# Casting x on GpSimd in place of VectorE, one slot sooner, with two of the four loads placed two slots behind the casts

## Chip, cores, metric

One Trainium2 chip, one core. The metric is device time in microseconds (us), the median of several executions. A profile is one further execution, and its span is about 1.8 us shorter than the time of the same run, as the time includes more than first to last instruction.

## The reference, cut to what matters

```python
# x: (8, 3008, 256) fp32
X = np.fft.rfft(x, axis=1)                       # along the 3008 positions
Y = X * (filt_r + 1j * filt_i)[None, :, :]
x = np.fft.irfft(Y, n=3008, axis=1).reshape(24064, 256)
h = np.maximum(x @ moe_w_in, 0.0)                # 256 -> 2048
out = h * h @ moe_w_out                          # 2048 -> 256
```

## The kernel before

The feed-forward part runs in groups of 512 tokens, 8 slots to a group. Into the slots of one batch the Fourier part of the next is woven: x is loaded, cast to fp16, transformed (psA), multiplied by the filter (psB to prod to yf), transformed back (psP), and later written out as yt (psY). TensorE works through all of this in program order; so does VectorE. I call the stretch from a batch's first psB to its last psP the **filter stage**; a *stage length* below is the time from one batch's first psB to the next batch's first psB, read from TensorE's timeline.

```python
def cast_x(b, c, eng=nc.vector):
    t = p_x16.tile([94, 8, D], F16, tag="x16", name=f"x16_{b}_{c}")
    eng.tensor_copy(out=t, in_=x32s.pop((b, c))[0:94])      # L340
    x16s[(b, c)] = t
...
def unit_b(b, p):                                # 12 units p in a batch
    ps = psF(f"psB_{b}_{p}")                     # psF: two PSUM buffers, for psA, psB, psP, psY
    ... two psB matmuls ...
    nc.vector.tensor_mul(out=prod, in0=ps (from PSUM), in1=sF[...])      # L453
    nc.vector.tensor_copy(out=yf[0:64], in_=prod[64:128, 1])             # L460
    nc.vector.tensor_copy(out=yf[64:128], in_=prod[0:64, 1])             # L461
def unit_s(b, p):
    nc.vector.tensor_add(out=yf, in0=prod[:, 0], in1=yf)                 # L467
def ffn_sq(g, s):                                # once in every slot
    nc.vector.tensor_mul(out=v, in0=v, in1=v)    # L570, h squared
...
def fft_plan(b):                                 # put(slot, place, function, ...)
    t0 = 14 if b == 1 else 19
    for p in range(12):
        r = t0 + (17 if b == 1 else 18) * p // 11
        put(r, 0, unit_b, b, p)
        put(r, 0, unit_s, b, p)
        put(r + 2, 1, unit_p, b, p)              # the psP pair that reads yf
    t0 = 34 if b == 1 else 40
    for c in range(4):
        put(t0, 1, read_z, b, c)                 # dZ -> zt, which psY needs
    if b + 1 < B:
        for c in range(2):
            put(t0 - 13, 1, load_x, b + 1, c)    # two input buffers x32
        for c in range(4):
            r = t0 - 8 + 3 * c
            put(r, 1, cast_x, b + 1, c)
            if c < 2:
                put(r, 1, load_x, b + 1, c + 2)
```

So batch 1's stage carries the casts of batch 2's x, and so on: six stages with four casts each.

## Time and profile before

| | before |
|---|---|
| time, median of 3 runs | 793.43 us (793.39 to 793.74) |
| profiled span | 791.9 us |
| stage length, batch 1; batches 2 to 6 | 92.39; 94.94 each |
| from the last batch's first psB to the start of the last psO | 147.80 us |
| VectorE busy, of it casts (L340) | 550.3 us, 29.2 |

How to read it: stages 2 to 6 agree to 0.01 us because TensorE streams in them without a wait. Whatever lengthens a stage is therefore TensorE waiting, and it can be read off stage by stage.

### The profile page before, as it was taken

What the parts mean: (1) busy time and instruction counts of PE and PEld (TensorE: products, weight loads), DVE (VectorE), ACT (ScalarE), POOL (GpSimd) and SP (SyncE); (2) the same over time, 40 slices, a digit from 0 to 9 for tenths busy, and PEclk for the clock granted to TensorE, in tenths of its full rate; (3) what the DMA queues carried; (4) which work ended last, traced back from release to release, by engine and by line L of the source; (5) the groups of instructions that cost most, each with busy time, mean ns of one, the idle gap of its engine ahead of it and who ended that gap; (6) DMA issues with size and microseconds to landing.
All of it is one profiled execution on the core that took longest, in us unless ns stands there. A gap on an engine that the chain in (4) does not pass through costs nothing.

```text
span 791.9 us, 14822 instructions
## 1 busy us (share of the span) xinstructions
PE 778.9 (98%) x6102; PEld 552.5 (70%) x6102; DVE 550.3 (69%) x897; ACT 557.4 (70%) x711; POOL 23.6 (3%) x36
## 2 busy tenths in 40 slices
PE   8989999999999999999999999999999999999998
PEld 5746667667676777867777676776767677676666
DVE  6866994579755897559965699556995579553342
ACT  3976776777777777767776777676777777776664
POOL 3800000000000000000000000000000000000000
PEclk9999999999999999999999999999999999999999
DMA  9994554346814557154562555424563332611111
GB/s 363 368 260 153 146 157 111 93 135 167 205 42 112 167 155 180 48 173 135 132 167 65 163 147 155 112 80 148 159 180 86 97 133 66 147 40 41 41 41 54
DMA packets 88571, 107.32 MB, mean 136 GB/s; under 512 B 6336, under 2 KB 79040, under 8 KB 84288
## 3 DMA queue, kind: packets, MB, share of 16 engines
q1 hardware_dynamic: 88296, 106.19, 46.5%
q8 instruction: 48, 0.79, 0.4%
q10 hardware_dynamic: 144, 0.18, 0.1%
q14 instruction: 19, 0.16, 0.1%
q0 software_dynamic: 64, 0.00, 0.0%
HBM read 58.12 MB, written 48.23 MB: 134 GB/s over the span
## 4 chain that ended last, share of the span: by engine, by line
PE 89%; DVE 6%; DMA 3%; ACT 1%; SPq 0%; issue 0%; DVEq 0%; ACTq 0%
PE psO L579 40%; PE psH L562 38%; PE psA L361 3%; PE psY L532 2%; PE psB L445 2%; DMA f<-in_filt_i_dram 2%; PE psP L496 2%; DVE prod L453 2%; DVE h L570 1%; DMA wout<-in_moe_w_out_dram 1%; PE psf L287 1%; PE psf L290 1%; DVE yf L467 0%; ACT sF L298 0%; DVE yf L461 0%; ACT h L566 0%
## 5 line engine op out<-in xcount | busy, mean ns | idle before, releaser
L566 ACT ACTIVATE h<-psH 128x1024 f16<-128x1024 f32 x376 | 384.9, 1024 | 189.3 <-PE psH L562 186.7
L579 PE MATMUL psO<-sWout,h 128*128 128x256 f16 x3008 | 388.9, 272 | 0.6 <-DVE h L570 0.6
L562 PE MATMUL psH<-yt,sWin 128*128 128x512 f16 (+7 forms) x1728 | 386.9, 351 | 1.6 <-DVE yt L541 0.7
L579 PEld LDWEIGHTS <-h 128*128 128x128 f16 x3008 | 290.6, 98 | 79.1 <-DVE h L570 0.9
L570 DVE TENSOR_TENSOR h<-h 128x1024 f16<-128x1024 f16 x376 | 252.6, 685 | 104.7 <-ACT h L566 104.5
L562 PEld LDWEIGHTS <-sWin 128*128 128x128 f16 x1728 | 159.5, 98 | 101.7 <-issue 3.3
L453 DVE TENSOR_TENSOR prod<-psB,sF 128x1024 f16<-128x1024 f32 x84 | 102.3, 1218 | 2.8 <-PE psB L445 2.8
L541 DVE CAST yt<-psY 128x376 f16<-128x376 f32 x62 | 34.0, 549 | 59.4 <-PE psY L532 59.4
L367 DVE CAST u<-psA 96x512 f16<-96x512 f32 x50 | 34.3, 687 | 47.3 <-PE psA L361 45.1
L498 ACT CAST ze<-psP 128x512 f16<-128x512 f32 x84 | 49.1, 585 | 17.2 <-PE psP L496 14.7
L590 ACT COPY ost<-psO 128x512 f32<-128x512 f32 (+1 forms) x96 | 55.8, 581 | 6.8 <-PE psO L579 5.3
L532 PE MATMUL psY<-sC,zt 112*128 112x94 f16 x512 | 42.4, 205 | 1.4 <-DMA zt<-dZ 1.4
L532 PEld LDWEIGHTS <-zt 112*128 112x128 f16 x512 | 35.1, 98 | 11.6 <-issue 1.6
L467 DVE TENSOR_TENSOR yf<-prod,yf 128x512 f16<-128x512 f16 x84 | 35.7, 425 | 2.9
L361 PE MATMUL psA<-x,sC 94*96 94x512 f16 x96 | 36.6, 382 | 0.0
L445 PE MATMUL psB<-ut,sSB 128*128 128x256 f16 x192 | 36.5, 273 | 0.0
L496 PE MATMUL psP<-yf,sSP 128*128 128x256 f16 x168 | 32.1, 272 | 0.5 <-DVE prod L453 0.3
L539 ACT CAST yt<-psY 128x376 f16<-128x376 f32 x66 | 30.9, 468 | 2.0 <-issue 1.7
L445 PEld LDWEIGHTS <-sSB 128*128 128x128 f16 x192 | 18.5, 98 | 19.5
L340 DVE CAST x<-x 94x2048 f16<-94x2048 f32 x24 | 29.2, 1216 | 0.0
L365 ACT CAST u<-psA 96x512 f16<-96x512 f32 x50 | 28.6, 572 | 0.0
L460 DVE COPY yf<-prod 64x512 f16<-64x512 f16 x84 | 24.3, 289 | 2.9
(65 smaller groups left out, 253.2 us busy)
## 6 DMA issues: line engine op xcount, KB each, us to landing
x<-in_x_dram SPq DMA_DIRECT2D x20, 768.0 KB
zt<-dZ SPq DMA_DIRECT2D x64, 192.0 KB
dU<-u SPq DMA_DIRECT2D x28, 384.0 KB
dZ<-ze SPq DMA_DIRECT2D x28, 384.0 KB
out_dram<-ost SPq DMA_DIRECT2D x66, 128.0 KB
out_dram<-ost SPq DMA_DIRECT2D x31, 256.0 KB
ut<-dU SPq DMA_DIRECT2D x7, 1024.0 KB
xw<-in_x_dram SPq DMA_DIRECT2D x6, 1024.0 KB
```

The source lines that it names most:

```text
L361: nc.tensor.matmul(ps[0:96, :], sSA, x16s[(b, c)][:, m, :], start=True, stop=True)
L445: nc.tensor.matmul(ps[:, i * D:(i + 1) * D], sSB[:, 2 * p + i, :], uts[b][:, 2 * p + i, :], start=True, stop=True)
L453: nc.vector.tensor_mul(out=prod, in0=ps.rearrange("p (a d) -> p a d", d=D).unsqueeze(1).to_broadcast([128, 2, 2, D]), in1=sF[:, :, 2 * p:2 ...
L467: nc.vector.tensor_add(out=yf, in0=prod[:, 0], in1=yf)
L496: nc.tensor.matmul(ps[:, i * D:(i + 1) * D], sSP[:, 2 * p + i, :], yf[:, i, :], start=True, stop=True)
L498: nc.scalar.copy(out=zes[(b, c)][:, 2 * i6:2 * i6 + 2, :], in_=ps.rearrange("p (a d) -> p a d", d=D))
L532: nc.tensor.matmul(ps[:, 94 * jj:94 * jj + 94], zt[:, 4 * (g % 2) + jj, dt * 128:(dt + 1) * 128], sSY, start=True, stop=True)
L562: nc.tensor.matmul(ps[:, i, o:o + n], sWin[:, dt, jt * 128:(jt + 1) * 128], yts[b][:, dt, r:r + n], start=(dt == 0), stop=(dt == 1))
L566: nc.scalar.activation(out=h2[:, 2 * s:2 * s + 2, :], in_=ps, func=AF.Relu)
L570: nc.vector.tensor_mul(out=v, in0=v, in1=v)
L579: nc.tensor.matmul(pso[g][:, t % 2, :], h2s[g][:, jt, t * 128:(t + 1) * 128], sWout[:, jt, :], start=(jt == 0), stop=(jt == NJT - 1))
L590: nc.scalar.copy(out=ost[:, h0:h0 + step, :], in_=pso[g][:, h0:h0 + step, :])
```

## The change

The intent: take 29 us of casts off VectorE, which is nearly full in the filter stage, and give them to GpSimd, which is idle after the first 40 us; and place the third and fourth loads so that SyncE no longer waits for a cast.

```diff
-    def cast_x(b, c, eng=nc.vector):
+    def cast_x(b, c, eng=nc.gpsimd):
...
             for c in range(4):
-                r = t0 - 8 + 3 * c
+                r = t0 - 9 + 3 * c
                 put(r, 1, cast_x, b + 1, c)
                 if c < 2:
-                    put(r, 1, load_x, b + 1, c + 2)
+                    put(r + 2, 1, load_x, b + 1, c + 2)
```

## The prediction

> **What bounds the kernel now.** I read the page's busy shares first, then TensorE's waits over the whole run, then its waits from 120 us on, then the busy time of each engine in one stretch, and last the timelines of VectorE, TensorE, GpSimd and SyncE around one set of casts.
>
> ```profile
> PE 778.9 (98%) x6102; PEld 552.5 (70%) x6102; DVE 550.3 (69%) x897; ACT 557.4 (70%) x711; POOL 23.6 (3%) x36
> ...
> L340 DVE CAST x<-x 94x2048 f16<-94x2048 f32 x24 | 29.2, 1216 | 0.0
> ...
> PE psH L562 <- DVE yt L541: 0.2, 1, 0.2
> ...
> 165.60:206.70 41.10, 41.10 (x298) 29.04 (x297) 39.71 (x71) 30.37 (x38) 0.00 (x0) 1.00 0.50 140
> 206.70:260.50 53.80, 53.80 (x440) 38.16 (x439) 30.11 (x48) 38.17 (x51) 0.00 (x0) 1.00 0.45 127
> ```
>
> The first line says TensorE is busy 98% of the span. The third is the entire answer to "what does TensorE wait for between 120 and 790 us": one wait of 0.2 us. In that stretch it streams without a gap: in its timeline the group of 8 psO products takes 0.87 us from its start to the next start, the group of 4 psH products the same, a psB or psP pair 0.22, and they follow each other exactly. So the end is set by TensorE, and there is next to nothing to win. The last two lines (columns: length, then busy TensorE, weight load, VectorE, ScalarE, GpSimd) add the one danger: in the 41.1 us in which batch 2's filter stage (psB to prod to yf to psP) runs, VectorE is busy 39.71 us, 97%; in the 53.8 us after it, only 56%. VectorE is a second bound that is almost reached once per batch, and that is where the x casts (line L340, 24 of 1.216 us) sit.
>
> How near is it? Here is VectorE around the casts of batch 3's x, and after it the TensorE pairs that wait for it:
>
> ```profile
> 183.84 0.42 DVE L467 TENSOR_TENSOR yf<-prod,yf 128x512 f16<-128x512 f16 x1
> 184.19 0.69 DVE L570 TENSOR_TENSOR h<-h 128x1024 f16<-128x1024 f16 x1
> 184.79 1.22 DVE L453 TENSOR_TENSOR prod<-psB,sF 128x1024 f16<-128x1024 f32 x1
> 186.04 0.29 DVE L460 COPY yf<-prod 64x512 f16<-64x512 f16 x1
> 186.34 0.29 DVE L461 COPY yf<-prod 64x512 f16<-64x512 f16 x1
> 186.66 0.42 DVE L467 TENSOR_TENSOR yf<-prod,yf 128x512 f16<-128x512 f16 x1
> ...
> 194.14 1.22 DVE L340 CAST x<-x 94x2048 f16<-94x2048 f32 x1
> ...
> 205.72 0.42 DVE L467 TENSOR_TENSOR yf<-prod,yf 128x512 f16<-128x512 f16 x1
> ...
> 188.67 0.38 PE L496 MATMUL psP<-yf,sSP 128*128 128x256 f16 x2
> ...
> 206.27 0.38 PE L496 MATMUL psP<-yf,sSP 128*128 128x256 f16 x2
> ```
>
> The yf that is added at 186.66 (ready at 187.09) is read by the psP pair at 188.67: a margin of 1.58 us. After two casts (194.14 and 201.51) the stage's last yf is ready at 206.15 and read at 206.27: 0.12 us is left. The same margins, to 0.02 us, come back in the stages at 281 to 301, 376 to 396, 471 to 491 and 566 to 586 us. So before the change the schedule just fits.
>
> **What the Trainium skill says.** "SBUF — State Buffer", section "Who interferes with whom": GpSimd has only VectorE's second port pair; it is an exclusive lock held for a whole instruction, against VectorE copies and casts in a two-port mode and against a VectorE operation with two SBUF inputs; an operation with one SBUF input outside those modes does not contend. "VectorE: DVE Perf Modes", section "Mode 2×_2P", gives that mode to single-source copies from SBUF to SBUF. The trace of before agrees where it can be tested, in the prologue:
>
> ```profile
> 11.61 0.69 DVE L222 CAST xw<-xw 128x1024 f16<-128x1024 f32 x1 [1.20 <-DMA xw<-in_x_dram]
> 11.64 1.56 POOL L222 CAST xw<-xw 128x1024 f16<-128x1024 f32 x1 [8.98 <-DMA xw<-in_x_dram]
> 20.49 1.04 POOL L222 CAST f<-f 128x1024 f16<-128x1024 f32 x1 [2.37 <-DMA f<-in_filt_i_dram]
> 20.56 1.51 DVE L222 CAST f<-f 128x1024 f16<-128x1024 f32 x1 [0.26 <-DMA f<-in_filt_i_dram]
> 24.42 7.06 DVE L453 TENSOR_TENSOR prods<-psB,sF 128x1024 f16<-128x1024 f32 x6
> 35.15 3.99 POOL L222 CAST xw<-xw 128x1024 f16<-128x1024 f32 x4
> ```
>
> At 11.6 VectorE came first by 0.03 us and GpSimd's 1.0 us cast took 1.56; at 20.5 GpSimd came first and VectorE's 0.69 us cast took 1.51, about the 0.8 us that it had to wait. The product from PSUM ran at 7.06/6 = 1.18 us beside GpSimd's copies, undisturbed. No pair of a tensor_tensor with two SBUF inputs (L467, L570) and a GpSimd operation is in this trace. "GPSIMD Engine Reference", section "Engine selection", has one-input work on GpSimd at roughly line rate; the trace agrees: 0.998 us for 1024 elements (3.99/4).
>
> **The change part by part.** *Removed:* 24 casts x 1.216 = 29.2 us of VectorE, four for each of six batches. At most they free the waits for VectorE up to 120 us: 0.59 us at 114.2 (psO for h, after a late chain of casts at 101 to 109) and 0.27 at 93.9, say 0.9 us together. After 120 us they free nothing, as there is no wait.
> *Added:* 24 casts on GpSimd. From 1024 elements at 0.998 us and 1504 at 1.41 (2.82/2), the slope is 0.86 ns per element, so 2048 take 0.998 + 1024 x 0.00086 = 1.88 us undisturbed (estimate). 24 x 1.88 = 45 us on an engine that was idle after 40 us: no bound by itself.
> *Moved:* on GpSimd the program slot no longer sets when a cast runs, since nothing else is queued there: it runs when its load lands. The first two loads are issued at 177.97 and just after (SyncE's timeline); their packets and semaphores land at about 184.2 and 186.8. So the first two casts move from 194.1 and 201.5 to about 184.3 and 186.8. The third load was issued at 195.38, on the end of the first VectorE cast; its buffer is now free since about 186, so SyncE passes it right after the output write of 191.5, and the fourth right after the dZ write of 197.5 instead of 202.75. "Two slots later" therefore means earlier or equal in time, and SyncE's 49 us of waits for L340 vanish (41.9 + 7.2 in its own waits). They were on no path, so this is worth nothing.
>
> *What the lock costs in one stage.* The first cast asks at 184.3 while L570 runs, gets the pair at 184.8 and holds it to 186.7. L453 (PSUM) is not held up until 186.0; then L460 waits 0.62 us, starting at 186.66. The second cast asks at 186.85 and gets the pair at the end of L460, at 186.95, to 188.83: L461 waits 1.87 us. The yf that had 1.58 us of margin is late by 0.62 + 1.87 - 1.58 = 0.9 us, and its psP pair, in order before everything else on TensorE, stalls it by about 1.0 us. The next units had margins of 2.07 and 2.27 us and now 1 us more, so no second stall. At 194 to 206 VectorE is without its two casts (-2.4 us) and gets two lock waits of 0.7 to 1.9 us: about even against the 0.12 us margin, which has grown by the earlier stall. So 1.0 us a stage, in the five stages of batches 2 to 6: 5 us. The stage of batch 1, whose first unit margins at 93 to 98 us are 2.2 to 2.9 us, costs 0 to 0.7.
> Sum: 793.4 - 0.9 + 0.4 + 5.0 = 798 us.
>
> **The rivals.** *The casts are hidden:* GpSimd asks for the pair while VectorE issues back to back, and if VectorE keeps it until its next product from PSUM, the hold of 1.88 us lies beside 1.22 us that needs no pair; only 0.66 us is lost per cast, 1.3 for two, under the 1.58 margin. Then nothing stalls: 793.4 - 0.9 = 792.5. For it: the prologue shows who came first, not who wins when VectorE's queue is full; and tensor_tensor may not block at all. Against it: the blocked casts there started as soon as the pair was free. *A worse lock:* each cast blocks VectorE for its full 1.88 us and the last unit's margin of 0.12 fails as well: another 1 to 1.5 us per stage, so 804. Against it: the prod, 42% of a unit's VectorE time (1.22 of 2.9 us), needs no pair. *x comes late for psA:* the fourth load would land at about 203 and psA needs it only in the next batch, 20 us later and more (the psA products of batch 3 start at 234); excluded. *VectorE was the bound and the 29 us show:* that would be 764; the empty list of waits excludes it.
>
> **Range and chances.** I give the lock with stalls (798) about 0.5, the hidden casts (792.5) 0.4, the worse lock (804) 0.1: 0.5 x 798 + 0.4 x 792.5 + 0.1 x 804 = 796.4. As either of the first two is likelier in a half measure than in full, I put the point at 795.5 us and the range at 792.0 to 801.0. Faster by 2% needs 777.6, under what TensorE streams: 0.01. Slower by 2% needs 809.3, that is 2.7 us in each of six stages: 0.04.
>
> **What would show it.** In the profile after: GpSimd at about 68 us (9%), the L340 group on POOL with a mean of 1.9 to 2.4 us; VectorE's L460, L461, L467 and L570 with means above 289, 289, 425 and 685 ns (the blocked ones), L453 unchanged; new TensorE waits of about 1 us, five times, of psP L496 on DVE L467, near 189, 284, 379, 474 and 569 us; SyncE's wait on L340 gone. It is wrong if VectorE's means do not move (no lock for tensor_tensor), if the waits stand near 206 us instead (the end of the stage), if the GpSimd cast is far longer than 1.9 us, or if no wait appears.

## More of the kernel before

The page's lines of VectorE's filter work, to be compared later (columns: busy us, mean ns of one, then idle before):

```profile
L570 DVE TENSOR_TENSOR h<-h 128x1024 f16<-128x1024 f16 x376 | 252.6, 685 | 104.7 <-ACT h L566 104.5
L467 DVE TENSOR_TENSOR yf<-prod,yf 128x512 f16<-128x512 f16 x84 | 35.7, 425 | 2.9
L460 DVE COPY yf<-prod 64x512 f16<-64x512 f16 x84 | 24.3, 289 | 2.9
```

## The result, and the profile after

805.22 us, median of 4 runs (803.43 to 806.85), against 793.59 for before on the same chip. The ratio is 1.0143, 95% interval 1.0117 to 1.0169. A ratio here is always the mean time of one kernel's runs over that of the other's in the same rounds, so not quite the ratio of the quoted medians. The change makes the kernel 1.4% **slower**: clear of the noise and above the predicted range (792.0 to 801.0).

| stage | before | after | longer by |
|---|---|---|---|
| batch 1 | 92.39 | 94.45 | 2.06 |
| 2 | 94.94 | 96.80 | 1.86 |
| 3 | 94.94 | 97.46 | 2.52 |
| 4 | 94.94 | 96.87 | 1.93 |
| 5 | 94.94 | 96.86 | 1.92 |
| 6 | 94.94 | 96.65 | 1.71 |
| rest, from the last batch's first psB | 147.80 | 147.80 | 0.00 |

The six stages that carry casts hold 12.0 us of it, two each; the rest, without a cast, holds nothing. The profiled spans differ by 13.1 us; the other 1.1 lie before the first stage, where this execution had 3.4 us of TensorE at half clock (granted 0.92 between 36 and 52 us, against 1.00). The profile of the kernel with late GpSimd casts (below), which is no slower than before, shows one as well (granted 0.96), so it is no part of the effect.

The page after, in answer to the lines above:

```profile
PE 784.0 (97%) x6102; PEld 552.3 (69%) x6102; DVE 553.0 (69%) x873; ACT 557.6 (69%) x711; POOL 72.0 (9%) x60
...
L570 DVE TENSOR_TENSOR h<-h 128x1024 f16<-128x1024 f16 x376 | 267.8, 725 | 116.3 <-ACT h L566 113.4
L453 DVE TENSOR_TENSOR prod<-psB,sF 128x1024 f16<-128x1024 f32 x84 | 102.2, 1217 | 1.5 <-PE psB L445 1.4
L340 POOL CAST x<-x 94x2048 f16<-94x2048 f32 x24 | 48.4, 2015 | 514.9 <-DMA x<-in_x_dram 482.9
...
L467 DVE TENSOR_TENSOR yf<-prod,yf 128x512 f16<-128x512 f16 x84 | 43.9, 523 | 2.9
...
L460 DVE COPY yf<-prod 64x512 f16<-64x512 f16 x84 | 29.2, 348 | 2.9
```

VectorE runs 24 instructions fewer (873 against 897) and is busy *longer*: 553.0 against 550.3 us. L570 grew by 15.2 us, L467 by 8.2, L460 by 4.9 and L461 by 1.6 (25.8 against 24.2): 29.9 us, or **1.25 us of VectorE time for each GpSimd cast, where its own cast had cost 1.216**. L453, which reads one operand from PSUM, did not move. GpSimd's cast takes 1.89 us undisturbed and 2.02 on average. Read cast by cast, each of the 24 overlaps exactly one VectorE operation that is over 0.1 us longer than the median of its kind: 11 L570, 7 L460, 5 L467 and 1 L461.

Now TensorE's waits over the whole run; the list of before has neither of these two (columns: total us, times, longest):

```profile
PE psB L445 <- DVE prod L453: 6.5, 8, 1.1
...
PE psP L496 <- DVE yf L467: 2.5, 4, 1.5
```

And the chain of one loss, batch 2's stage, from the timelines of GpSimd, VectorE and TensorE:

```profile
187.58 2.19 POOL L340 CAST x<-x 94x2048 f16<-94x2048 f32 x1 [71.84 <-DMA x<-in_x_dram]
190.41 2.02 POOL L340 CAST x<-x 94x2048 f16<-94x2048 f32 x1 [0.64 <-DMA x<-in_x_dram]
...
189.19 0.73 DVE L460 COPY yf<-prod 64x512 f16<-64x512 f16 x1
...
190.59 2.98 DVE L570 TENSOR_TENSOR h<-h 128x1024 f16<-128x1024 f16 x2
193.50 1.21 DVE L453 TENSOR_TENSOR prod<-psB,sF 128x1024 f16<-128x1024 f32 x1
...
196.91 1.22 DVE L453 TENSOR_TENSOR prod<-psB,sF 128x1024 f16<-128x1024 f32 x1
...
198.18 0.38 PE L445 MATMUL psB<-ut,sSB 128*128 128x256 f16 x2 [1.08 <-DVE prod L453]
```

Both casts start when their loads have landed, not in their slots. Counted from the stage's first psB (165.64 before, 168.78 after), they stand at 18.8 and 21.6 us, where VectorE had run them at 28.5 and 35.9 (194.14 and 201.51). The first holds L460 up by 0.44 us; the second catches one of two L570 operations (2.98 us for the two, against 1.29). The prod that should follow at once starts at 193.50; its psB had ended at 191.10. Two units later the tenth unit's psB, one slot behind the ninth's, finds its buffer still being read by the prod of 196.91 to 198.13, and TensorE stands. The line gives 1.08 us of idle time; a pair that does not wait begins 0.17 us before the modelled end of the one in front, so this wait costs the stage 1.25 us. Before, the same prod ran from 191.91 to 193.13 and that psB started at 193.66, with 0.53 us to spare:

```profile
191.91 1.23 DVE L453 TENSOR_TENSOR prod<-psB,sF 128x1024 f16<-128x1024 f32 x1 [0.20 <-PE psB L445]
...
193.66 0.38 PE L445 MATMUL psB<-ut,sSB 128*128 128x256 f16 x2
```

### The profile page after: what moved, and what is told of

It is laid out like the page before. It is cut to its first block, busy times and chain, and to the rows that moved or that the text cites. A ratio compares the mean times of both kernels' runs of the same rounds, so it can differ in the third digit from the quotient of the medians.

```text
span 805.0 us, 14863 instructions
## 1 busy us (share of the span) xinstructions
PE 784.0 (97%) x6102; PEld 552.3 (69%) x6102; DVE 553.0 (69%) x873; ACT 557.6 (69%) x711; POOL 72.0 (9%) x60
## 4 chain that ended last, share of the span: by engine, by line
PE 71%; DVE 26%; ACT 1%; issue 1%; DMA 1%; ACTq 0%; DVEq 0%; SPq 0%
PE psO L579 30%; PE psH L562 30%; DVE prod L453 9%; DVE h L570 8%; DVE yf L467 4%; DVE yf L460 3%; PE psA L361 3%; PE psY L532 3%; DVE yf L461 2%; PE warm L268 1%; PE psB L445 1%; PE psP L496 1%; PE psf L287 1%; PE psf L290 1%; ACT sF L298 0%
## 5 line engine op out<-in xcount | busy, mean ns | idle before, releaser
L570 DVE TENSOR_TENSOR h<-h 128x1024 f16<-128x1024 f16 x376 | 267.8, 725 | 116.3 <-ACT h L566 113.4
L453 DVE TENSOR_TENSOR prod<-psB,sF 128x1024 f16<-128x1024 f32 x84 | 102.2, 1217 | 1.5 <-PE psB L445 1.4
L340 POOL CAST x<-x 94x2048 f16<-94x2048 f32 x24 | 48.4, 2015 | 514.9 <-DMA x<-in_x_dram 482.9
L467 DVE TENSOR_TENSOR yf<-prod,yf 128x512 f16<-128x512 f16 x84 | 43.9, 523 | 2.9
L532 PEld LDWEIGHTS <-zt 112*128 112x128 f16 x512 | 35.1, 98 | 11.2 <-issue 1.2
L445 PE MATMUL psB<-ut,sSB 128*128 128x256 f16 x192 | 36.5, 272 | 6.5 <-DVE prod L453 6.5
L460 DVE COPY yf<-prod 64x512 f16<-64x512 f16 x84 | 29.2, 348 | 2.9
```

Of the source, the lines that this page charges most:

```text
L445: nc.tensor.matmul(ps[:, i * D:(i + 1) * D], sSB[:, 2 * p + i, :], uts[b][:, 2 * p + i, :], start=True, stop=True)
L453: nc.vector.tensor_mul(out=prod, in0=ps.rearrange("p (a d) -> p a d", d=D).unsqueeze(1).to_broadcast([128, 2, 2, D]), in1=sF[:, :, 2 * p:2 ...
L532: nc.tensor.matmul(ps[:, 94 * jj:94 * jj + 94], zt[:, 4 * (g % 2) + jj, dt * 128:(dt + 1) * 128], sSY, start=True, stop=True)
```

## The experiments

In the sketches of edits, "after" is the changed kernel. Where a kernel has added lines in `cast_x`, later line numbers are higher by 2 (L570 becomes L572). Losses of a stage are given for batches 2 to 6 against 94.94 us.

The theory after seeing the result: **GpSimd's cast holds the SBUF port pair of the prediction's lock, which VectorE's copies and two-input operations need, so VectorE loses as much time as its own cast had cost, but in lumps of up to 1.9 us and earlier in the stage, where a psB or psP has less margin.** Rivals: the moved loads and slots; any fixed cost of work on GpSimd; the mere removal of the casts from VectorE's order.

### All but the engine

```diff
 after:
-    def cast_x(b, c, eng=nc.gpsimd):
+    def cast_x(b, c, eng=nc.vector):
```

> The whole change but the engine: the casts one slot sooner and the loads two slots after them, on VectorE as before. Theory (GpSimd's casts hold VectorE's second port pair beside the filter stage): within 1.5 us of before, 792 to 795, filter stages of 94.9 us. Rival (the moved loads or the sooner casts cost it): about 805, stages of 96.8.

Measured: 797.0 us, ratio 1.0035 (1.0017 to 1.0052). Stage 1 lost 0.70 us, most of it at a psO that waits for h (1.08 us, 0.59 before), and each later one 0.36, at the tenth unit's psB (five waits for prod of 0.2 us). The time missed my 792 to 795 by 2 us: a VectorE cast one slot sooner stands just ahead of the tight pair of units. But it is about a quarter of the 11.6 us, so slots and loads aren't the main cause.

### The engine alone

```diff
 before:
-    def cast_x(b, c, eng=nc.vector):
+    def cast_x(b, c, eng=nc.gpsimd):
```

> The engine alone: GpSimd casts, loads and casts in the slots of before. Theory: 803 to 808 as with the whole change, because on GpSimd a cast runs when its load lands and the slot does not matter; blocked VectorE operations of 1.9 to 2.2 us in the filter stage. Rival (loads): about 793.5.

Measured: 808.77 us, ratio 1.0177 (1.0154 to 1.0199). Stages 2 to 6 lost 1.9 to 3.3 us, 1.25 of it again at the tenth unit's psB. At 808.8 it is just above my 803 to 808. The engine does it, with the old slots as with the new. L453 stayed at 1217 ns, L570 rose to 721 and L460 to 405.

### GpSimd casts behind the filter stage

```diff
 after:
             for c in range(2):
-                put(t0 - 13, 1, load_x, b + 1, c)
+                put(t0 - 3, 1, load_x, b + 1, c)
             for c in range(4):
-                r = t0 - 9 + 3 * c
-                put(r, 1, cast_x, b + 1, c)
+                put(t0 + 1 + c, 1, cast_x, b + 1, c)
                 if c < 2:
-                    put(r + 2, 1, load_x, b + 1, c + 2)
+                    put(t0 + 1 + c, 1, load_x, b + 1, c + 2)
```

> All casts on GpSimd, but all four loads later (the first two 10 slots, to 3 slots before the dZ reads, the others behind the casts), so that no cast runs beside the filter stage. Theory in its full form (the lock costs only where VectorE has no idle time): 791.5 to 794, though single VectorE operations still are stretched by up to 1.9 us. Rival (a GpSimd cast costs TensorE about 0.5 us wherever it stands, 12 us in 24): about 805.

Measured: 793.41 us, ratio 0.9993 (0.9975 to 1.001). No filter stage lost anything. Yet VectorE was held up again: it is busy for 546.9 us where 521.1 would be left without the casts, and L570's mean is 743 ns, more than in the changed kernel. Around two casts behind batch 2's stage

```profile
208.89 1.89 POOL L340 CAST x<-x 94x2048 f16<-94x2048 f32 x1 [70.52 <-DMA x<-in_x_dram]
211.16 1.92 POOL L340 CAST x<-x 94x2048 f16<-94x2048 f32 x1 [0.38 <-DMA x<-in_x_dram]
...
209.53 4.68 DVE L570 TENSOR_TENSOR h<-h 128x1024 f16<-128x1024 f16 x3 [1.38 <-ACT h L566]
```

three L570 operations take 4.68 us, where three take 1.88 undisturbed, and no TensorE wait follows. So there is no fixed price of a GpSimd cast: the same hold-up is free where VectorE has idle time. The last cast-carrying stage was 95.57 us, as psY waited 0.5 us for zt: the x loads now stand near the zt reads.

### The control for it: the late slots on VectorE

```diff
 before:  (loads and slots as in the run above, eng=nc.vector)
```

> The late slots and loads of the run with late GpSimd casts, but on VectorE: the control for it. Theory: 792 to 794, as behind the filter stage VectorE is 56% busy; so the late place, not the engine, decides. If it is slower than 795, VectorE's casts harm there and GpSimd would be worth something in that place.

Measured: 865.07 us, ratio 1.0912 (1.0891 to 1.0932). My expectation was far off, and the run is no control for the lock. VectorE's waits show why:

```profile
DVE x L340 <- DMA x<-in_x_dram: 76.1, 13, 13.2
```

VectorE works in order, so a cast whose load has not landed stops all that stands behind it, up to 13.2 us at a time, and TensorE's psY and psH wait for VectorE's yt (44.5 and 11.2 us). In each stage the trace also has 10.2 to 13.7 us of half clock around the long wait, and TensorE's busy time is 793.2 us, 14.3 more than before. GpSimd, with an otherwise empty queue, waited 509.8 us for loads in the run above at no cost. In these late slots that is worth 71.7 us; the kernel before loads so early that it does not need it.

### The casts on ScalarE

```diff
 before:
-        eng.tensor_copy(out=t, in_=x32s.pop((b, c))[0:94])
+        nc.scalar.copy(out=t, in_=x32s.pop((b, c))[0:94])
```

> The casts on ScalarE, in the slots and with the loads of before: VectorE loses the same 29 us[...]. Theory: no VectorE operation is stretched, and the time is at or under before, 792 to 794, unless ScalarE's queue (74% busy in the filter stage, a cast of about 2 us) delays the Relu that frees psH; then a wait for ScalarE, not VectorE, shows, up to 798. Rival (taking the casts from VectorE's queue is itself harmful, as h and prod come in another order): 800 and more with waits for VectorE.

Measured: 795.4 us, ratio 1.0016 (0.9999 to 1.0032). The casts took 1.914 us each on ScalarE; L467 and L570 stayed at 425 and 685 ns; VectorE's busy time fell by 25.0 us, to 525.3; no filter stage had a new wait (35.84 us from first to last psB, as before). The 0.17 us that each stage lost lie outside it, and 795.4 against a range of 792 to 794 is a small miss. Relieving VectorE does no harm in itself; it just gains nothing, as TensorE was streaming anyway.

### Only the first two, only the last two

```diff
 after:
-                put(r, 1, cast_x, b + 1, c)
+                put(r, 1, cast_x, b + 1, c, nc.gpsimd if c < 2 else nc.vector)   # first two
+                put(r, 1, cast_x, b + 1, c, nc.vector if c < 2 else nc.gpsimd)   # last two
```

> Only the first two casts of a batch on GpSimd, the last two on VectorE (slots and loads of the change). In the changed kernel the first pair cost 1.4 of the 1.9 us of a stage. Theory: 800 to 804, the wait again of psB on prod in the middle of the stage. Rival (each of the 24 casts costs the same): half of the 12 us, 799.5.

Measured: 801.08 us, ratio 1.0095 (1.008 to 1.011). Stages 2 to 5 lost 1.4 to 2.3 us, mostly 1.25 at the tenth psB; stage 6 only 0.28, as the casts there met VectorE at another moment. As expected.

> Only the last two casts on GpSimd, the first two on VectorE (slots and loads of the change). The sooner first VectorE cast alone cost 0.36 us a stage in the run with the change but the engine; the third cast cost 0.5 in the changed kernel, the fourth nothing as the stage is then over. Theory: 796 to 800, below the run with the first two. Rival (all casts the same): 799.5 and more.

Measured: 806.98 us, ratio 1.0164 (1.0139 to 1.0189). A clear miss: half of the casts on GpSimd cost as much as all. (The profiled execution, 801.9 us, was one of the quicker ones.) VectorE in batch 2's stage:

```profile
198.37 2.38 DVE L570 TENSOR_TENSOR h<-h 128x1024 f16<-128x1024 f16 x1
200.67 1.21 DVE L340 CAST x<-x 94x2048 f16<-94x2048 f32 x1
```

The third cast, on GpSimd from 198.04, holds up L570, and directly behind it comes VectorE's own second cast: both delays in a row, and 1.24 us lost at the eleventh unit's psP in every stage from 1 to 6. In the changed kernel the same GpSimd cast met a VectorE that was rid of its own casts. The stretched operations run 1.69 us over their kinds' medians for each GpSimd cast here, and 1.07 in the run with the first two. The costs of the casts do not add up; they depend on what else stands in the queue.

### Twice the cast

```diff
 after:
-        eng.tensor_copy(out=t, in_=x32s.pop((b, c))[0:94])
+        x32 = x32s.pop((b, c))
+        for _ in range(2):
+            eng.tensor_copy(out=t, in_=x32[0:94])
```

> The changed kernel with each GpSimd cast made twice, so the port pair is held twice as long and nothing else is added to VectorE or TensorE. Theory: the cost grows by more than itself, 818 to 835, with blocked VectorE operations of 2 us twice as often. Rival (the cost comes from VectorE's new order or from the earlier loads): stays at 803 to 808.

Measured: 841.75 us, ratio 1.0581 (1.0527 to 1.0634), even above my range. Nothing was added but 24 GpSimd casts, and each cost 1.5 us of the whole (36.5 over 24). Stages 2 to 6 took 100.3 to 105.4 us. Not all of it is waiting: each stage also has 3.4 us at half clock (10.2 in the first), which the changed kernel's stages have not, and TensorE's busy time is 11.4 us above the changed kernel's (795.4 against 784.0).

### Read or write: memset against cast

```diff
 before, the VectorE cast kept:
+        nc.gpsimd.memset(x32[0:94], 0.0)                  # memset run
+        nc.gpsimd.tensor_copy(out=t, in_=x32[0:94])       # recast run
```

> The kernel before, all casts kept on VectorE, and behind each one a GpSimd memset over the spent input tile (94x2048 fp32, estimated 1.8 us from 0.52 us for 512 elements). It writes SBUF and reads nothing. The Trainium skill has an operation with two SBUF inputs contend only with a GpSimd operation that reads: then L467 and L570 stay at 425 and 685 ns, only the copies L460 and L461 (and casts L340) are stretched, and the time is 794 to 800. If any GpSimd operation blocks all of them, L570 is stretched too and the time is nearer to the next run.

> The twin of the memset run: the kernel before with all VectorE casts kept, and behind each one the same cast made once more on GpSimd, so nothing is taken off VectorE and the pair is held 24 times 1.9 us for reading and writing. Theory: L467 and L570 are stretched as in the changed kernel, and with VectorE's own 29 us still there the cost is above that of the change: 806 to 818. If the cost of the change came from anything but the held pair (order, loads), this stays near 794.

Measured: memset 793.89 us, ratio 1.0005 (0.9988 to 1.0022); recast 813.26 us, ratio 1.0255 (1.0239 to 1.027). The GpSimd operations take 1.80 us and, on average, 2.2, and stand behind the same VectorE casts. Beside a memset, 48 L570 operations overlap one by more than 0.1 us and none is stretched (679 to 693 ns); for instance

```profile
202.79 1.80 POOL L342 MEMSET x<- 94x2048 f32 x1 [5.57 <-DVE x L341]
...
202.60 1.28 DVE L572 TENSOR_TENSOR h<-h 128x1024 f16<-128x1024 f16 x2
```

two of them take 1.28 us, as ever. In the recast run 18 of 41 are stretched, up to 2.37 us, and every stage from 2 to 6 is 3.2 us longer (98.17). So it is GpSimd's *reading* of SBUF that holds up the two-input operations, not its being busy, as the expectation of the memset run had it from the Trainium skill, "SBUF — State Buffer", section "Who interferes with whom". I had expected the memset to stretch the copies L460 and L461. It did not (290 ns), but only six overlap one, at its very end, so whether a write holds up a copy is left open.

### The cast in eight pieces

```diff
 after:
-        eng.tensor_copy(out=t, in_=x32s.pop((b, c))[0:94])
+        x32 = x32s.pop((b, c))
+        for m in range(8):
+            eng.tensor_copy(out=t[:, m, :], in_=x32[0:94, m, :])
```

> The changed kernel with each GpSimd cast cut into 8 of 94x256 (an estimated 0.34 us each from 0.998 us for 1024 elements and the slope of 0.86 ns). If the pair is held for one instruction, no VectorE operation is stretched by more than about 0.4 us, and pieces also run beside the products from PSUM: 796 to 803. If the pair were held as long as GpSimd has work, or if GpSimd's total time counted, it is as slow as the change or slower, 805 to 812.

Measured: 794.59 us, ratio 1.0015 (1.0 to 1.003), better than my range. GpSimd is busy far longer (117.0 us against 72.0, as its pieces wait), VectorE shorter (535.8 against 553.0):

```profile
185.11 0.39 DVE L463 COPY yf<-prod 64x512 f16<-64x512 f16 x1
185.54 0.50 DVE L469 TENSOR_TENSOR yf<-prod,yf 128x512 f16<-128x512 f16 x1
185.96 1.68 DVE L572 TENSOR_TENSOR h<-h 128x1024 f16<-128x1024 f16 x2
```

No operation is stretched by more than 0.24 us; pieces and VectorE operations take turns. A stage lost 0.39 us, all at the tenth psB, and the first stage was 0.76 us *shorter* than before (91.63). A whole cast held an operation up by as much as 1.7 us, the pieces none by more than 0.24: the hold lasts one instruction, and its size sets the damage.

### Two tries for a better version, and the tight pair

```diff
 pieces placed: pieces, and in place of the change's plan
+            for c in range(2):
+                put(t0 - 8, 1, load_x, b + 1, c)
+            for c in range(4):
+                put(t0 - 6 + 2 * c, 1, cast_x, b + 1, c)
+                if c < 2:
+                    put(t0 - 3 + c, 1, load_x, b + 1, c + 2)
```

> A try for a better version than both: GpSimd casts in 8 pieces, the first two loads five slots later, so that the pieces run at the end of the filter stage where VectorE's own casts stood and the tight psB pair at its middle is past. Theory: no stage over 94.95 us, the first stage 0.8 us under before: 792.6, against 793.4 before, which may not be clear of the noise. If pieces cost VectorE more than the 1.2 us of its own cast, the last yf of a stage (0.12 us margin) stalls and it is 794 to 796.

Measured: 803.71 us, ratio 1.0131 (1.0113 to 1.0149). The filter stages lost nothing at all, as hoped, but:

```profile
PE psY L534 <- DMA zt<-dZ: 8.7, 5, 2.5
```

The x loads now stand close ahead of the zt reads in the one DMA queue, and psY waits for zt. One of the five waits, 1.1 us, lies in the prologue, where before has one too; the other four, 7.6 us, are new. Stage 6 lost 4.3 us for a wait of 2.5, as 3.4 us at half clock follow it there. A new wait in another place ate it.

```diff
 spread: after, or after with pieces
-            r = t0 + (17 if b == 1 else 18) * p // 11
+            r = t0 + (17 if b == 1 else 18) * p // 11 + (b > 1 and p == 9)
```

> The changed kernel with one filter unit moved: the tenth of a batch (its psB, prod and yf) one slot later in batches 2 to 7. In the changed kernel this unit's psB, one slot behind the ninth's, waits 1.25 us for the ninth's prod in nearly every stage, two thirds of a stage's loss. If that close pair is what turns held-up VectorE work into TensorE time, the 1.25 goes and a stage loses 0 to 0.8 us instead of 1.9: 795 to 799. If VectorE simply lacks the time, the stall moves to the next unit and the time stays at 803 to 807.

Measured: 803.9 us, ratio 1.0121 (1.0094 to 1.0148). The rival was right: the 1.25 us at the tenth psB went, and up to 0.76 came at the eleventh's instead, with other waits in other stages (11 waits of psB for prod, 5.3 us in all); stages 2 to 6 lost 0.6 to 3.6, 9.0 together against 9.9, and the intervals of the two kernels' ratios overlap. The close pair is where the delay shows, not what makes it.

> The casts in 8 pieces on GpSimd and the tenth unit one slot later: the pieces alone lost 0.39 us a stage, all at that unit's psB. Theory: that goes, all stages at 94.94, the first 0.8 us under before: 792.2 to 793.0, at or just under before. Rival: the stall moves on, 794 to 795 as with the pieces alone.

Measured: 793.52 us, ratio 0.9991 (0.9978 to 1.0005). With the smaller delays of the pieces, the spread did help: stages at 94.94 to 95.00, the first at 92.03. It is above my 792.2 to 793.0 all the same: this and the late GpSimd casts are at the time of before, not under it. No version here beats it: TensorE streams, and no cast on any engine changes what it has to do.

## Why the prediction was wrong, point by point

- **What bounds the kernel:** right. Every lost microsecond is a TensorE wait inside one of six stages; the stretch without casts kept its 147.80 us.
- **No gain from freeing VectorE:** right and shown (ScalarE casts, late casts: no faster than before). The 0.9 us that I allowed for batch 1's stage is real only where nothing holds VectorE up: 0.76 us came with the pieces and with the late casts; under the change that stage lost 2.06.
- **A cast runs when its load lands:** right; that is why slots did little (the engine alone, 808.8). But the fourth load was not issued sooner, behind the dZ write (32 us into the stage): it went at 37.7 us, behind an output write, against 37.1 before. Its cast stands past the stage's last psP and cost TensorE nothing. SyncE's waits for L340 fell from 49.1 to 0.4 us, as said.
- **The lock:** right, and now shown for L467 and L570 (stretched up to 2.15 and 2.38 us), of which the trace of before had no example. The duration estimate, 1.88 us, measured 1.89.
- **The delay of VectorE:** right in size, partly by luck. I worked out 0.62 + 1.87 = 2.49 us for the first two casts, 1.25 each; measured over all 24, 29.9 us, 1.25 each. In stage 2 the first two cost 0.44 + 1.69 = 2.13 us, and the second met L570, not the L461 that I named.
- **The step that failed** is the next one: "The yf that had 1.58 us of margin is late ... stalls it by about 1.0 us. The next units had margins of 2.07 and 2.27 us and now 1 us more, so no second stall." That stall did not come in four of the five stages. In stage 2 the second cast asked at 21.6 us after the stage's first psB, not at 21.2, and this unit's copies were through by then. In those four stages its psP kept a margin of 0.9 to 1.1 us; only in stage 3, where the casts met L460 and L467, did the stall come (1.48 us). Behind it I followed the delay through the psP products alone. psB also waits for VectorE, for the prod that empties its buffer, and the tenth psB's margin was 0.53 us. The delay arrived there: 1.25 us in stages 2, 4, 5 and 6 of the changed kernel, 0.75 in stage 3. "At 194 to 206 ... about even" failed too: the third cast cost 0.5 us more at the tenth unit's psP in stages 2, 4 and 5. That psP had 0.49 us of margin before, next after the 2.07 and 2.27 that I read, and I passed over it. So the term "1.0 us a stage, in the five stages" measured 1.99 on average (9.94 over 5), and the first stage's "0 to 0.7", less 0.9, measured 2.06. With these in place of mine, 793.4 + 9.9 + 2.1 = 805.4, against 805.2 measured (the profiled execution itself took 806.85, with the 1.1 us before its first stage).
- **The rivals:** "the casts are hidden" (0.4) was wrong for whole casts, though nearly what the pieces do. "A worse lock" came to 804, close by number but not by reason: a cast did not block VectorE for its full 1.88 us, and it was not the stage's last margin of 0.12 us that failed.
- **What would show it:** VectorE's means rose and L453 stayed, as said; GpSimd was busy for 72.0 us rather than 68. Of the five psP waits near 189, 284 and so on only the 1.5 us wait in stage 3 resembles what came; most were psB waits, some 9 us later in the stage.

What stays open: why the runs scatter (803.4 to 806.9 for the change on one chip, where before lies within 2.5 us on any chip; the run with placed pieces scatters by 3.8, so it isn't whole casts alone). The casts start with the landing of their loads, and stage 3 lost 0.6 us more than its neighbours with casts elsewhere in the same pattern, which fits, but I did not test it.

## What to carry to other kernels

Moving work to an idle engine may not relieve the busy one, as here, where the one's casts held up the other's operations: add up the busy one's stretched operations, and compare with what was taken away (here 29.9 us against 29.2). If the idle engine is used all the same, cut its instructions small, or put them where the other has idle time, and check every buffer that waits for the delayed engine, not just the nearest. And where TensorE already streams, ask first what there is to win: here it was under 1 us.

## What the Trainium skill lacked or had wrong

- "SBUF — State Buffer" advises, in its summary of rules for kernel authors, to schedule whichever of the two is off the critical path. It lacks the remedy of cutting the GpSimd instruction: eight pieces of 94x256 took turns with VectorE and stretched no operation by more than 0.24 us, and the kernel went from 1.0143 to 1.0015 of the time of before.
- The same page says, under "Who interferes with whom", that who issues first decides. It lacks who wins when VectorE issues without a pause: GpSimd got the pair between two operations of a full queue. Its 24 whole casts took 1.892 to 2.427 us, so none waited more than 0.54 us, less than one L570; in the run with the last two, one took 2.97 us, behind a VectorE cast.
- "GPSIMD Engine Reference", section "Engine selection", calls one-input work roughly line rate: the cast of 2048 elements took 1.89 us, against 1.216 on VectorE and 1.914 on ScalarE, so on fp32 to fp16 casts between SBUF tiles GpSimd is 1.55 times VectorE's time. The page has no such figure for a cast.
